# A vector of 2048 words loaded as 16 rows and turned on TensorE, in an attention and feed-forward kernel whose order a planner makes

## The chip, the core and the metric

The kernel runs on one core of one Trainium2 chip. The metric is the device time of one execution in microseconds (us); smaller is better. Three timed executions of the kernel before have a median of 761.31 us.

## What is computed

Soft-capped attention over 4 batches of 12 heads, 448 rows and 64 columns each, then a feed-forward layer with a leaky rectifier whose slope `alpha` is a vector of 2048 float32 words, one for each hidden column.

```
scores = cap * tanh(q @ k.T / sqrt(64) / cap)        # per batch and head
attn   = exp(scores - max) / (sum + 1e-9)
x      = attn @ v, heads side by side                 # (1792, 768)
h      = x @ w_in                                     # (1792, 2048)
g      = max(h, 0) + alpha * min(h, 0)
out    = g @ w_out                                    # (1792, 768)
```

## The kernel before

The work goes through four batches. The first batch's attention (`attention32`) runs in float32; its two query parts of 192 and 256 rows a head are taken one after the other for six pairs of heads, in units. The later batches (`attention`) run in pairs of float16 numbers, high and low part, with DMA transposes for the turned tiles. The products with w_in (`mm1`, line 741) and w_out (`mm2`, line 782) follow batch by batch. While the first batch's attention runs, w_in and w_out come in as 8-byte words in 16 chunks each, are turned into float32 by VectorE (lines 837, 841, 847), measured by a product with themselves (`norms`, line 861) and split into two float16 parts.

No queue is written out by hand. Each step is handed to `Plan.op` with a priority number, the engines that can do it with a time for each, and the regions that it reads and writes. `Plan.order` then plays the kernel through at build time: whenever an engine is free it takes the ready step with the least number, and the order in which the steps start there is the order in which each engine's queue gets them. For a DMA the three numbers are SyncE's time to issue it, the time from issue to the transfer, and the time for which the one transfer lane is held; the transfers are played one behind the other in that lane, and 1000 ns later a transfer has landed. The play begins at 1230 ns. A load of q, k or v has (500, 1900, 1000) ns, a load of w_in (500, 1900, 3400).

Where the play finds TensorE idle before a set time, it puts an empty product into the queue (`fill`, line 991), a 128 by 128 float16 product whose result nobody reads. On the chip these run in their place in the queue, whatever the chip then has to do.

A step that needs one of four PSUM banks takes it through a handle. A handle of kind "n" serves the small turns and maxima, and only one of that kind is held at a time.

`alpha` comes in by `g_scales`, called with priority 30 between the loads of the first batch and its attention. The tile `alph` holds word j*128+p in partition p, column j. From it `absmax` (line 345) takes a maximum per partition, `allmax` turns that column on TensorE (line 362), takes the maximum over the row (line 358) and spreads it back over the partitions by a product (line 365); `g_scale` makes the factors `sg`, `cs_g` and `ca_g` from it, which `mm1` applies to its products in the two steps behind each (lines 381 or 383, then 751). All steps of this chain share the region "sg", and so run in order.

Of the kernel before, what the change touches and what calls it, by code (L numbers as in the profile page):

```python
# [10 lines left out]
F32 = mybir.dt.float32  # L11
# [64 lines left out]
class Plan:  # L76
# [15 lines left out]
    def op(self, prio, times, fn, r=(), w=(), rows=1.0, port=True):  # L92
        o = lambda: None
        o.prio, o.times, o.fn, o.rows, o.idx, o.port = prio, times, fn, rows, len(self.ops), port
        o.handles, deps = [], set()
        for write, regions in ((False, r), (True, w)):
            for x in regions:
                if isinstance(x, Handle):
                    if x not in o.handles:
                        o.handles.append(x)  # L100
                        x.ops.append(o)
                    x = (x, 0, 1)
                space, lo, hi = x
                old = self.acc.setdefault(space, [])
                deps.update(e[2] for e in old if e[0] < hi and lo < e[1] and (write or e[3]))
                if write:
                    old[:] = [e for e in old if e[0] < lo or hi < e[1]]
        for write, regions in ((False, r), (True, w)):
            for x in regions:
                space, lo, hi = (x, 0, 1) if isinstance(x, Handle) else x  # L110
                self.acc[space].append((lo, hi, o.idx, write))
        o.deps = len(deps)
        o.next = []
        for d in deps:
            self.ops[d].next.append(o)
        self.ops.append(o)
        return o
# [120 lines left out]
def kernel(  # L238
# [11 lines left out]
    nc = tc.nc  # L250
    B, H, S, D = q.shape
    DM, DFF = w_in.shape
    P = 128
# [6 lines left out]
    NF = DFF // P  # L260
# [7 lines left out]
    def ct(shape, dt, name):  # L268
        return const.tile(shape, dt, tag=name, name=name)

    ps_s = [psum.tile([P, 2, 512], F32, tag=f"s{i}", name=f"s{i}") for i in range(2)]
    ps_p = [psum.tile([P, 512], F32, tag=f"p{i}", name=f"p{i}") for i in range(4)]
# [3 lines left out]
    amz = [small[:, i:i + 2] for i in (8, 10)]  # L276
    joint = ct([P, B // 2], F32, "joint")
    alph = ct([P, NF], F32, "alph")
    n_wi = ct([P, NF], F32, "n_wi")
    iv_wi = ct([P, NF], F32, "iv_wi")  # L280
    s_wi = ct([P, NF], F32, "s_wi")
# [2 lines left out]
    sg = ct([P, NF], F32, "sg")  # L284
# [31 lines left out]
    ident, identr = ct([P, P], F32, "ident"), ("ident", 0, 1)  # L316
# [11 lines left out]
    plan = Plan()  # L328
    op = plan.op
# [14 lines left out]
    def absmax(o, i):  # L344
        nc.vector.tensor_reduce(out=o, in_=i, axis=AX.X, op=ALU.max, apply_absolute_value=True)
# [3 lines left out]
    def allmax(prio, src, rows, r, first, w):  # L349

        h = plan.handle("n")
        m, at = src.shape[-1], mxt_no[0]
        mxt_no[0] += 1 + m if m > 1 else 1
        top, diag = mxt[:m, at:at + 1], mxt[:m, at + 1:at + 1 + m]
        tr = (("mxt", at), 0, 1)

        def reduce(e):
            nc.vector.tensor_reduce(out=top, in_=ps_p[h.slot][:m, :rows], axis=AX.X, op=ALU.max)
            if m > 1:
                nc.vector.tensor_scalar(out=diag, in0=ident[:m, :m], scalar1=top, scalar2=None, op0=ALU.mult)  # L360

        op(prio, {"pe": 150}, lambda e: nc.tensor.transpose(ps_p[h.slot][:m, :rows], src, ident[:rows, :rows]),
           r=[*r, identr], w=[h])
        op(prio, {"dve": 480 if m > 1 else 260}, reduce, r=[h], w=[tr], port=False)
        op(prio, {"pe": 100}, lambda e: nc.tensor.matmul(  # L365
            ps_p[h.slot][:, 256:256 + m], ones[:m], diag if m > 1 else top, start=True, stop=True), r=[tr], w=[h])
        op(prio, {"dve": 150}, lambda e: first(ps_p[h.slot][:, 256:256 + m]), r=[h], w=w, port=False)
# [548 lines left out]
            split_w(WT_P + WT_S * j, wo[j], room_r(wo_room[j]), room[j], room_r(j), s_wo[:, j:j + 1], ("s_wo", 0, 1), share(j, AO))  # L916

    def g_scales(prio):
        op(prio, {"sp": (500, 1100, 900)}, lambda e: nc.sync.dma_start(out=alph, in_=alpha.rearrange("(j p) -> p j", p=P)), w=[("sg", 0, 1)])
        op(prio, {"dve": 80}, lambda e: absmax(c_g, alph), w=[("sg", 0, 1)])  # L920
        allmax(prio, c_g, P, [("sg", 0, 1)], lambda top: nc.vector.tensor_scalar(
            out=c_g, in0=top, scalar1=1.0, scalar2=2.0 ** 20, op0=ALU.max, op1=ALU.mult), [("sg", 0, 1)])
        op(prio, {"dve": 1130}, g_scale, w=[("sg", 0, 1)])
# [42 lines left out]
    def all_ops():  # L966
        loads32()
        g_scales(30)
        for part in range(2):
            for pair in range(NPAIR):  # L970
                attention32(part, pair)
        for j in range(0, NF, WG):
            w_in_chunks(j, WG)
        for part in range(2):
            mm1_batch(0, *PART[part], part)
        w_out_all()
        out_scale(0)
        for b in range(1, B + 1):
            if b < B:
                vbatch(b)  # L980
                for pair in range(NPAIR):
                    attention(b, pair)
                out_scale(b)
            mm2_batch(b - 1)
            if b < B:
                mm1_batch(b, 0, S, 0)
# [52 lines left out]
```

## Time and profile before

| | |
|---|---|
| median of three timed executions | 761.31 us (761.2 to 761.73) |
| the profiled execution, its own time | 763.0 us |
| span of its trace | 761.1 us |
| mean granted TensorE clock in the span | 0.983 of full |
| instructions | 14048 |
| DMA packets | 227940, of which 191457 under 512 B |

The span goes from the first to the last instruction in the trace; the execution's own time has some 1.9 us around it. Busy time is the time in which an engine runs instructions; waiting, branching and issuing DMAs are not counted. A granted clock of 1.00 is 2.4 GHz, and TensorE's lower level is 1.2 GHz.

### The profile page before, as it was taken

The numbers are of one execution on the slowest core, as the hardware profiler recorded it, in microseconds if no ns is written. First come the engines' busy times: TensorE is split into PE (matmuls) and PEld (weight loads), VectorE is DVE, ScalarE is ACT, GpSimd is POOL, SyncE is SP. The second block draws the span as 40 slices with busy tenths as digits, with TensorE's granted clock in tenths as the row PEclk, the third lists the DMA queues.
The fourth block names the chain that finished last, engine by engine and source line by source line (L and its number), as shares of the span: only waits on it lengthen the run. The fifth ranks groups of instructions, "written<-read, shape, count | busy, mean of one in ns | idle before, by whom it ended". The sixth has DMA issues, their size and how long they took to land.

```text
span 761.1 us, 14048 instructions
## 1 busy us (share of the span) xinstructions
PE 736.8 (97%) x5332; PEld 464.8 (61%) x5332; DVE 511.1 (67%) x1146; ACT 452.4 (59%) x903; POOL 125.8 (17%) x197
## 2 busy tenths in 40 slices
PE   9999989989888999999999999999999999999997
PEld 6866666668776876566555555555555555555664
DVE  3787888998877798867778787877877701543000
ACT  3567778787675687767767666767776500332010
POOL 1010110124333110211433300012233000000000
PEclk9999989999998999999999999999999999999999
DMA  8984441868885836898867599999765721000001
GB/s 212 253 235 125 129 163 55 266 155 157 193 168 102 155 75 142 185 183 153 141 126 132 117 187 213 180 177 159 134 121 93 121 54 39 1 0 1 22 22 42
DMA packets 227940, 98.71 MB, mean 130 GB/s; under 512 B 191457, under 2 KB 224161, under 8 KB 227873
## 3 DMA queue, kind: packets, MB, share of 16 engines
q1 hardware_dynamic: 227872, 97.82, 62.2%
q8 instruction: 42, 0.69, 0.4%
q14 instruction: 26, 0.20, 0.1%
HBM read 45.82 MB, written 5.51 MB: 67 GB/s over the span
## 4 chain that ended last, share of the span: by engine, by line
PE 83%; DVE 5%; DMA 4%; ACT 4%; issue 2%; POOL 0%; SPq 0%; ACTq 0%; POOLq 0%
PE p L782 28%; PE p L741 24%; PE s L724 5%; PE p L596 5%; PE p L991 5%; PE s L665 4%; PE p L560 4%; DMA ptall<-pw 3%; PE p L610 2%; PE p L455 2%; DVE mxs L513 1%; PE p L861 1%; PE p L365 1%; PE p L454 1%; DVE pw L389 1%
## 5 line engine op out<-in xcount | busy, mean ns | idle before, releaser
L741 PE MATMUL p<-xring,wi 128*128 128x448 f16 (+2 forms) x1440 | 230.0, 319 | 1.9 <-DVE gr L751 1.9
L782 PE MATMUL p<-wp,gall 128*128 128x384 f16 x1344 | 225.2, 326 | 0.0
L741 PEld LDWEIGHTS <-wi 128*128 128x128 f16 x1440 | 138.4, 100 | 87.1 <-issue 5.0
L782 PEld LDWEIGHTS <-gall 128*128 128x128 f16 x1344 | 129.8, 98 | 89.3 <-issue 4.3
L520 ACT ACTIVATE tall<-tall,mxs,small 128x448 f32<-128x448 f32 x126 | 94.2, 749 | 14.9 <-POOL mxs L515 14.7
L515 POOL TENSOR_SCALAR mxs<-mxs,small 128x2 f32<-128x2 f32 (+1 forms) x93 | 45.9, 493 | 319.0 <-DVE mxs L513 202.1
L389 DVE SCALAR_TENSOR_TENSOR pw<-tall,rr,pw 128x448 f16<-128x448 f32 x126 | 85.5, 688 | 17.6 <-ACT pw L381 17.4
L386 POOL TENSOR_TENSOR gall<-gr,gall 128x384 f16<-128x384 f32 (+4 forms) x80 | 66.6, 842 | 167.2 <-ACT gall L375 101.6
L381 ACT ACTIVATE pw<-tall,rr 128x448 f16<-128x448 f32 x98 | 63.1, 660 | 43.7 <-DMA ptall<-pw 39.6
L751 DVE SCALAR_TENSOR_TENSOR gr<-p,ca_g,gr 128x448 f32<-128x448 f32 (+2 forms) x80 | 46.6, 585 | 54.0 <-ACT gr L381 53.7
L513 DVE TENSOR_REDUCE mxs<-tall 128x2 f32<-128x896 f32 (+1 forms) x72 | 69.0, 961 | 5.3 <-ACT tall L508 4.8
L508 ACT ACTIVATE tall<-s,ams 128x896 f32<-128x896 f32 (+1 forms) x72 | 64.8, 903 | 10.8 <-DVE pw L389 6.1
L724 PE MATMUL s<-qkTs 128*128 128x448 f16 (+1 forms) x288 | 61.4, 360 | 6.3 <-ACT tall L508 6.2
L381 ACT ACTIVATE gr<-p,cs_g 128x448 f32<-128x448 f32 (+2 forms) x60 | 32.9, 549 | 53.2 <-PE p L741 48.8
L381 ACT ACTIVATE wp<-p,small 128x384 f32<-128x384 f32 x23 | 13.3, 580 | 75.0 <-PE p L782 74.9
L991 PE MATMUL p<-ident 128*128 128x128 f16 x790 | 52.8, 224 | 2.2 <-POOL ident masks.py:199 1.7
L991 PEld LDWEIGHTS <-ident 128*128 128x128 f16 x790 | 48.3, 100 | 6.5 <-issue 2.4
L375 ACT ACTIVATE gall<-gr 128x384 f16<-128x384 f32 (+4 forms) x85 | 35.8, 434 | 25.3 <-DVE gr L751 25.0
L596 PE MATMUL p<-ptall,vs 112*64 112x448 f16 (+1 forms) x456 | 47.7, 350 | 1.6 <-issue 1.4
L724 PEld LDWEIGHTS <-qkTs 128*128 128x128 f16 (+1 forms) x288 | 22.3, 101 | 28.8 <-issue 15.6
L596 PEld LDWEIGHTS <-vs 112*64 112x64 f16 x456 | 25.9, 110 | 21.2 <-issue 7.5
L665 PE MATMUL s<-tall,qkTs 128*128 128x448 f32 x84 | 38.6, 589 | 0.0
(142 smaller groups left out, 828.6 us busy)
## 6 DMA issues: line engine op xcount, KB each, us to landing
wp<-in_moe_w_in_dram SPq DMA_DIRECT2D x16, 768.0 KB, 6.7
wp<-in_moe_w_out_dram SPq DMA_DIRECT2D x16, 768.0 KB, 4.7
rvs<-in_v_dram SPq DMA_DIRECT2D x38, 224.0 KB, 3.1
rqk<-in_q_dram SPq DMA_DIRECT2D x18, 224.0 KB, 3.0
rqk<-in_k_dram SPq DMA_DIRECT2D x18, 224.0 KB, 3.3
ptall<-pw SPq DMA_TRANSPOSE x148, 3.3
wp<-in_k_dram SPq DMA_DIRECT2D x6, 224.0 KB, 10.2
wp<-in_q_dram SPq DMA_DIRECT2D x6, 224.0 KB, 10.3
```

What stands on the lines that cost most here:

```text
L381: nc.scalar.activation(out=o, in_=i, func=AF.Copy, scale=s)
L386: (nc.gpsimd if e == "pool" else nc.vector).tensor_tensor(out=o, in0=a, in1=b, op=ALU.subtract)
L389: nc.vector.scalar_tensor_tensor(out=o, in0=i, scalar=s, in1=hi, op0=ALU.mult, op1=ALU.subtract)
L508: op(pr, {"act": 245 + 377 * m}, lambda e, s=s, t=t, m=m: nc.scalar.activation(out=t, in_=s[:, :m, :S].rearrange("p c (j k) -> p c j k", j ...
L513: op(pr, {"dve": 136 + 469 * m}, lambda e, mt=mt, t=t: nc.vector.tensor_reduce(out=mt, in_=t, axis=AX.XY, op=ALU.max), r=tr, w=[mr], port= ...
L520: nc.scalar.activation(out=t[:, x], in_=t[:, x], func=AF.Exp, scale=capt, bias=mt[:, x:x + 1], accum_out=u.sums[:, c:c + 1])
L596: nc.tensor.matmul(pv[x * D:(x + 1) * D, :n], vs[:, z, c:c + D], u.pt[x][:CP, y * NCH + kc], start=(i == 0), stop=(i == len(prods) - 1))
L665: steps(u, prio, n, lambda s, c: nc.tensor.matmul(s, qz[:, c * P:(c + 1) * P], kt[:, pair], start=True, stop=True), lambda c: 750, [qr, kt ...
L724: nc.tensor.matmul(s[rows], qT[:, x * S + cols.start:x * S + cols.stop], qkT[:, r0:r0 + NCH, :], start=(z == 0), stop=(z == 1))
L741: nc.tensor.matmul(ps_p[h.slot][:, :n], w[:, z, kk, :], x[:, d, o:o + n], start=(kk == 0 and z == d), stop=(kk == NPAIR - 1 and z == 1))
L782: nc.tensor.matmul(ps_p[h.slot][:, :NH], g[j][:, d, t * P:(t + 1) * P], w[:, z, hf * NH:(hf + 1) * NH], start=(j == 0 and z == d), stop=(j ...
L991: nc.tensor.matmul(ps_p[slot][:, :P], ident.bitcast(F16)[:, :P], ident.bitcast(F16)[:, P:], start=True, stop=True)
```

## The change

The load of `alpha` takes it as 16 rows of 128 words, each contiguous in memory, into a new tile `arow` of 16 partitions. A new TensorE step turns this tile into a PSUM bank of kind "n" against a 16 by 16 corner of the identity, and a new VectorE step copies the 128 by 16 result to `alph`. What follows is the same. The planner's numbers for the load change from (500, 1100, 900) to (500, 1900, 100), and the two new steps have 100 and 190 ns. The constants of the planner stay.

```diff
@@ -276,6 +276,7 @@
     alph = ct([P, NF], F32, "alph")
+    arow = ct([NF, P], F32, "arow")
@@ -916,7 +917,10 @@
     def g_scales(prio):
-        op(prio, {"sp": (500, 1100, 900)}, lambda e: nc.sync.dma_start(out=alph, in_=alpha.rearrange("(j p) -> p j", p=P)), w=[("sg", 0, 1)])
+        op(prio, {"sp": (500, 1900, 100)}, lambda e: nc.sync.dma_start(out=arow, in_=alpha.rearrange("(j p) -> j p", p=P)), w=[("arow", 0, 1)])
+        h = plan.handle("n")
+        op(prio, {"pe": 100}, lambda e: nc.tensor.transpose(ps_p[h.slot][:, :NF], arow, ident[:NF, :NF]), r=[("arow", 0, 1), identr], w=[h])
+        op(prio, {"dve": 190}, lambda e: nc.vector.tensor_copy(alph, ps_p[h.slot][:, :NF]), r=[h], w=[("sg", 0, 1)], port=False)
         op(prio, {"dve": 80}, lambda e: absmax(c_g, alph), w=[("sg", 0, 1)])
```

## Rows read from the trace of the kernel before

**Rows 1.** The page's table of busy us, share of the span and instructions.

```profile
PE 736.8 (97%) x5332; PEld 464.8 (61%) x5332; DVE 511.1 (67%) x1146; ACT 452.4 (59%) x903; POOL 125.8 (17%) x197
```

**Rows 2.** Busy us by stage: stretch, length, engines, granted clock, DMA share, GB/s.

```profile
40.00:80.00 40.00, 40.00 (x298) 26.70 (x297) 30.52 (x70) 28.72 (x62) 3.83 (x9) 1.00 0.63 179
80.00:160.00 80.00, 75.23 (x530) 53.10 (x530) 70.67 (x149) 66.44 (x138) 8.77 (x13) 0.94 0.51 152
160.00:240.00 80.00, 67.97 (x648) 55.80 (x645) 66.78 (x150) 56.99 (x128) 28.73 (x38) 0.91 0.78 161
...
360.00:600.00 240.00, 239.17 (x1456) 127.60 (x1454) 189.73 (x427) 168.26 (x334) 60.60 (x90) 1.00 0.81 147
```

**Rows 3.** The same for the empty products of line 991 alone (products, weight loads).

```profile
0.00:40.00 40.00, 16.47 (x224) 14.82 (x224) 1.00 1.00 233
...
160.00:240.00 80.00, 3.83 (x48) 3.46 (x48) 0.91 0.78 161
240.00:280.00 40.00, 17.64 (x288) 16.59 (x288) 1.00 0.67 120
```

**Rows 4.** Timeline of SyncE's queue: start us, us of the issue, line, out<-in.

```profile
2.52 0.46 SPq L825 DMA_DIRECT2D wp<-in_moe_w_in_dram  x1
3.03 0.55 SPq L919 DMA_DIRECT2D alph<-in_moe_alpha_dram  x1
3.62 4.31 SPq L399 DMA_DIRECT2D wp<-in_k_dram  x1
```

**Rows 5.** DMA packets of the stretches 6 to 7, 7 to 8, 8 to 9 us.

```profile
DMA packets 343, 0.35 MB, mean 351 GB/s; under 512 B 0, under 2 KB 343, under 8 KB 343
...
DMA packets 1758, 0.13 MB, mean 135 GB/s; under 512 B 1633, under 2 KB 1758, under 8 KB 1758
...
DMA packets 494, 0.05 MB, mean 50 GB/s; under 512 B 447, under 2 KB 494, under 8 KB 494
```

**Rows 6.** DMA issues of 1.3 to 3.7 us: KB, us from issue to landing.

```profile
small<-in_cap_dram SPq DMA_DIRECT2D x1, 0.5 KB, 3.3
...
alph<-in_moe_alpha_dram SPq DMA_DIRECT2D x1, 8.0 KB, 6.2
...
wp<-in_k_dram SPq DMA_DIRECT2D x1, 224.0 KB, 7.0
```

**Rows 7.** Timeline of alpha's readers and of VectorE ahead of them.

```profile
8.72 0.35 DVE L377 COPY qkTs<-p 64x192 f32<-64x192 f32 x1 [4.09 <-PE p L455]
...
11.81 0.16 DVE L345 TENSOR_REDUCE small<-alph 128x1 f32<-128x16 f32 x1
...
12.35 0.27 PE L362 MATMUL p<-ident,small 128*1 128x128 f32 x1
...
18.14 0.17 DVE L936 TENSOR_TENSOR ca_g<-alph,cs_g 128x16 f32<-128x16 f32 x1
```

**Rows 8.** Instructions on the tile cs_g: ns least/median/most, first and last start us.

```profile
L381 ACT ACTIVATE gr<-p,cs_g x60: 399/626/636, 158.7 to 694.5; 128x448 f32<-128x448 f32 x34, 128x192 f32<-128x192 f32 x13, 128x256 f32<-128x256 f32 x13
```

**Rows 9.** The chain that ended last, 8 to 14 us: start us, us, what.

```profile
12.07 0.45 PE p L991 x8
12.52 0.11 PE p L362
12.63 0.22 PE p L991 x4
```

**Rows 10.** The same chain, its five long waits for a transfer, 130 to 247 us.

```profile
132.93 4.87 DMA rqk<-in_k_dram
...
195.54 3.25 DMA rqk<-in_q_dram
...
205.26 3.76 DMA ptall<-pw
...
221.62 8.06 DMA ptall<-pw
...
241.72 4.58 DMA ptall<-pw
```

## The prediction

> **What bounds the kernel now.** I read the page's busy table first: TensorE is busy for 736.8 of 761.1 us and no other engine for more than 511.1 [rows 1]. The reader is to see a kernel bound by TensorE, with 24.3 us in which it does nothing (761.1 less 736.8). That share is a mean over unlike stages, so the table by stage comes next [rows 2]. TensorE is full in 40 to 80 us, leaves 4.8 us of 80 to 160 idle (80 less 75.23) and 12.0 of 160 to 240 (80 less 67.97), and has 239.17 of 240 us in 360 to 600. In 80 to 240 VectorE is the busiest engine but for one (70.67 of 80, then 66.78), and TensorE's granted clock is 0.94 and 0.91, so part of that time ran at 1.2 instead of 2.4 GHz. Late in the kernel nothing but TensorE's own queue of products counts.
>
> "Full" has to be taken with care. The planner puts empty products (line 991) wherever its plan has TensorE idle, a fixed number of them, and they cost their time on the chip whether or not there is still a gap. They hold 16.47 us of the first 40 us, 3.83 of 160 to 240 and 17.64 of 240 to 280 [rows 3]. So in the first 40 us TensorE's time is set by the plan: a gap that the plan no longer sees is what shortens it, not a transfer that lands sooner by itself.
>
> Alpha's own place is read from SyncE's queue, the DMA rates and the landing times. Alpha is the fifth DMA, issued at 3.03, and the next one, a load of k, holds SyncE for 4.31 us where the two issues ahead of it took 0.46 and 0.55 [rows 4]. The engines move 0.35 MB between 6 and 7 us, then 0.13 and 0.05 in the next two, while 1633 and 447 packets of under 512 B pass [rows 5]. Those 2080 small packets are alpha's 2048 words and some odds and ends. Alpha lands 6.2 us after its issue, at 9.2, the k load behind it at 10.6, 7.0 after its issue [rows 6].
>
> Its readers are read from the timeline. The first, VectorE's maximum, runs at 11.81, 2.6 us after the landing; the chain ends with the scaled alpha at 18.14 [rows 7], and the first use of a table that it makes is at 158.7 [rows 8]. Nothing on TensorE waits for alpha, then, nor for the k load: the turn of k follows at 12.85 (12.63 and 0.22), 2.2 us after that landing, and ahead of it in the chain that ended last stand 8 and 4 empty products, 0.45 and 0.22 us [rows 9].
>
> **The change, part by part.** *Removed: 2048 words as packets of their own.* At the 0.35 MB of the undisturbed us, the two us in question lost (0.35 less 0.13) and (0.35 less 0.05), over 0.35: 0.63 and 0.86, together 1.5 us of the DMA engines. The lower end counts the second us only by its share of the small packets, 447 to 1633 of the first: 0.63 times 1.27, 0.8 us. So each load behind alpha can land 0.8 to 1.5 us sooner. TensorE waits for none of them there, so by itself this is worth nothing.
>
> *Added: a load of 16 rows of 512 B.* The nearest row below is the smallest load, cap, 3.3 us from issue to landing; above, the scattered load itself, 6.2 [rows 6]. Alpha then lies in SBUF between 6.3 and 9.2 us.
>
> *Added: one TensorE turn of 16 by 128 and one VectorE copy of 128 by 16.* For the turn I take the turn of alpha's maxima, 0.27 us busy and 0.11 of the chain [rows 7, 9]; the copy stands between the maximum over the same 128 by 16 words, 0.16, and the copy of 64 by 192 out of PSUM, 0.35 [rows 7], and I take 0.16, for the size. In the plan the turn takes the place of empty products. If it doesn't, it costs 0.11 to 0.27. The copy falls where VectorE has little to do: it was idle for 4.09 us ahead of 8.72 [rows 7]. Cover gone, both cost 0.43 (0.27 and 0.16). The queue behind the new turn is that of TensorE's scores and turns; it would stand still if alpha landed after the turn is due. The plan makes it due no earlier than its own landing time for alpha: the start of 1230 ns, 1900 and 1000 for the first k load, 1000 for q, 3400 for w_in, 100 for alpha and 1000 for the landing, 9.63 us, which is 0.4 us after the latest landing I allow. So I put no wait there. The whole chain grows by these two steps and the way between them, some 1 us, against the 140 us until that first use.
>
> *Moved: the planner's clock for every later load.* In the plan alpha held the transfer lane for 900 ns and now holds it for 100. While that lane is the limit, every load behind it is due 0.8 us sooner in the plan. These are the kernel's own figures, no time of the chip. What the chip gets from them is fewer empty products: those ahead of the k turn, 0.45 and 0.22 us, are the ones that this can take away, 0.67 us, and the transfers give it the room, since they really come 0.8 us sooner at least. A second time it can't be had: a shift that is won at 12.85 is the same shift afterwards. I bound the direct effect by 0.8 us gained (the plan's whole shift) and 0.4 lost (nothing shifted, both new steps on the path), and take 0.67 gained.
>
> *Moved without being touched: the order of everything else.* The planner takes whichever ready step has the least priority number at each moment. With other due times in the first 40 us, other pairs meet on VectorE, ScalarE and SyncE, and the queues may come out otherwise up to 280 us. What this is worth the trace of before can't show. Its nearest rows are the five long waits for a transfer in the chain between 130 and 247 us: 4.87, 3.25, 3.76, 8.06 and 4.58 us [rows 10], on the mean 4.9. Each of them hangs on when SyncE came to issue one transfer.
>
> The profiled execution took 763.0 us for a span of 761.1, so 1.9 lie around the span; the sum against it is 763.0 less 0.67, 762.3. It stands 1.7 above the median of the three timed runs, 761.31, and the change is taken off that: 760.6.
>
> **The rivals.** *Hidden anyway, and no shift.* The readers of alpha come 2.6 us after the landing, the k turn 2.2 us after its own; if the plan was limited there by the scores and not by the loads, no empty product goes. Then the two steps are all that is left: 761.31 and at most 0.43, 761.7. Against it: 12 empty products stand right ahead of the k turn. The Trainium skill has this rule (DMA: Bandwidth & Descriptors, Rules for kernel authors): issue a DMA early and wait for it late, and its set-up cost lies beside the compute. By that rule too the old load cost nothing, and the change would not pay; the late reader in the trace agrees with it.
>
> *Slower: one more long wait between 130 and 247 us.* TensorE has few empty products to spare there (3.83 us in 160 to 240), and VectorE, which feeds the transposing transfers, has little room. If the new order puts one such transfer's issue behind another step on SyncE, another wait of the mean size comes on top: 760.6 and 4.9, 765.5. In 160 to 240 the granted clock is 0.09 short of full, which over 80 us is 7.2 us of work at full clock; a quarter more of that adds 1.8, 767.3. It decides once TensorE's idle time of 80 to 280 grows by over 2.2 us, which eats the 0.67 and passes the bound of a measurable change (0.2%, 1.5 us).
>
> *Faster: one such wait goes.* The same rows the other way: 760.6 less 4.9 is 755.7; less the longest, 8.06, it is 752.6. For it speaks that loads of the next batch's q and k, which two of the five waits name or follow, come sooner; against it that they come after 40 us, when the DMA share has fallen to 0.63 [rows 2] and the head start may have gone.
>
> **How the numbers follow.** Direct effect alone 0.33 (its own range 760.5 to 761.7), hidden anyway 0.05, slower 0.32, faster 0.30. The first two lie within 0.2%, so the same has 0.38. The time is that of the direct effect, 760.6. The range goes to one mean wait on the fast side, 755.7, and one mean wait with its clock on the slow side, 767.3, which leaves out about 2 in 10 between the two ends.
>
> **What would show it.** Packets of under 512 B nearly gone from 7 to 9 us, with some 0.3 MB moved in each; the k load behind alpha issued in about 0.5 us; alpha landed by 9.2; its turn near 10 to 12 us with no wait on TensorE; the k turn at about 12.2 with fewer empty products ahead. After 280 us the same stretches, shifted. The prediction is wrong if TensorE's idle time of 80 to 280, or its count of empty products, moves by more than 2 us: then the order decided, not alpha.

## The result, and the profile after

The changed kernel has a median of 768.36 us over 4 runs (766.63 to 770.64) against 761.52 for the kernel before (4 runs, 761.2 to 761.73): a ratio of 1.0092, 95% interval 1.0064 to 1.012. It is slower by some 6.8 us, where 760.6 was forecast and the range ended at 767.3. The profiled execution took 770.64 us for a span of 768.8.

Alpha's own part went as planned. The lines numbered here stand 1 to 4 below those of the kernel before (a product with w_out is L783, an empty product L995). First SyncE's queue, start and us of each issue, the counterpart of [rows 4]:

```profile
3.03 0.54 SPq L920 DMA_DIRECT2D arow<-in_moe_alpha_dram  x1
3.62 0.42 SPq L400 DMA_DIRECT2D wp<-in_k_dram  x1
```

then the DMA packets of 7 to 8 and of 8 to 9 us, for [rows 5]:

```profile
DMA packets 353, 0.32 MB, mean 319 GB/s; under 512 B 34, under 2 KB 353, under 8 KB 353
...
DMA packets 284, 0.27 MB, mean 271 GB/s; under 512 B 19, under 2 KB 284, under 8 KB 284
```

and the landing times of the two loads, for [rows 6]:

```profile
wp<-in_k_dram SPq DMA_DIRECT2D x1, 224.0 KB, 5.6
arow<-in_moe_alpha_dram SPq DMA_DIRECT2D x1, 8.0 KB, 5.5
```

The k load behind alpha is issued in 0.42 us instead of 4.31 and lands at 9.2 (3.62 and 5.6) instead of 10.6. Of the 2080 packets of under 512 B in these two us, 53 are left.

The new steps in the timeline (for [rows 7]), and the chain that ended last (for [rows 9]):

```profile
14.49 0.23 PE L922 MATMUL p<-ident,arow 16*128 16x16 f32 x1
...
16.20 0.16 DVE L923 COPY alph<-p 128x16 f32<-128x16 f32 x1
```

```profile
11.72 0.75 PE s L666 x2
12.47 0.10 PE p L455
12.57 0.34 PE p L456 x2
...
15.83 2.23 PE p L995 x38
```

The turn costs 0.23 us, the copy 0.16. The k turn (L455) follows the scores with no empty product between them, but behind the turns stand 38 of them where there were 27. From the first scores to the second TensorE runs 38 empty products in all, where it ran 39 (8, 4 and 27): they have moved, they have not gone.

What was lost is in the stages. Busy us, for [rows 2]:

```profile
40.00:80.00 40.00, 38.27 (x311) 28.35 (x311) 29.26 (x68) 25.74 (x56) 2.90 (x7) 0.96 0.49 144
80.00:160.00 80.00, 73.77 (x566) 53.99 (x565) 71.83 (x151) 62.10 (x128) 5.17 (x13) 0.98 0.49 149
160.00:240.00 80.00, 67.88 (x599) 53.54 (x599) 66.89 (x145) 61.41 (x134) 22.79 (x36) 0.89 0.82 164
240.00:280.00 40.00, 38.30 (x428) 31.67 (x427) 31.67 (x69) 27.04 (x55) 10.42 (x15) 1.00 0.60 127
```

and the empty products alone, for [rows 3]:

```profile
0.00:40.00 40.00, 15.19 (x210) 13.82 (x210) 1.00 0.93 254
40.00:80.00 40.00, 4.28 (x62) 3.67 (x62) 0.96 0.49 144
80.00:160.00 80.00, 4.90 (x75) 4.44 (x75) 0.98 0.49 149
160.00:240.00 80.00, 1.44 (x20) 1.27 (x20) 0.89 0.82 164
240.00:280.00 40.00, 10.15 (x164) 9.59 (x165) 1.00 0.60 127
```

The first 40 us have 1.3 us less of them. Then TensorE is idle in 40 to 80 (1.7 us, before none), and from 80 to 160 it is idle for 6.2 instead of 4.8 us and holds empty products too, of which there were none. So it is the middle of the kernel that has changed, tens of us behind alpha's last reader. The page's first table, for [rows 1]:

```profile
PE 738.4 (96%) x5351; PEld 469.1 (61%) x5351; DVE 520.8 (68%) x1143; ACT 458.3 (60%) x907; POOL 116.4 (15%) x197
```

TensorE's idle time in the whole span is 30.4 us (768.8 less 738.4) against 24.3. The empty products take 53.3 against 52.8, so its real work takes 685.1 against 684.0. Of the 7.7 us between the two spans, 6.1 are idle time, 0.5 empty products and 1.1 real work.

A milestone shows where. The first product with w_out, in the instructions of its line (ns least, median, most; first and last start in us), starts at 278.6 before and at 290.8 after:

```profile
L782 PE MATMUL p<-wp,gall x1344: 323/326/337, 278.6 to 756.5; 128*128 128x384 f16 x192
```

```profile
L783 PE MATMUL p<-wp,gall x1344: 323/326/337, 290.8 to 763.8; 128*128 128x384 f16 x192
```

12.2 us are lost by then, and 4.5 of them come back behind it, where the empty products hold less than before.

The five long waits of [rows 10] have changed with the order. Those of over 3 us between 120 and 280 us are now

```profile
167.89 3.09 DMA rvs<-in_v_dram
175.39 3.07 DMA ptall<-pw
183.00 6.56 DMA rqk<-in_q_dram
199.65 4.27 DMA rvs<-in_v_dram
264.82 6.76 DMA ptall<-pw
```

together 23.8 us against 24.5, so the loss is not one more of them.

### The profile page after: what moved, and what is told of

Its sections match the earlier page's. It is cut to its first block, busy times and chain, and to the rows that moved or that the text cites. A ratio compares the mean times of both kernels' runs of the same rounds, so it can differ in the third digit from the quotient of the medians.

```text
span 768.8 us, 14096 instructions
## 1 busy us (share of the span) xinstructions
PE 738.4 (96%) x5351; PEld 469.1 (61%) x5351; DVE 520.8 (68%) x1143; ACT 458.3 (60%) x907; POOL 116.4 (15%) x197
## 4 chain that ended last, share of the span: by engine, by line
PE 84%; DMA 7%; DVE 4%; ACT 3%; issue 1%; POOL 0%; ACTq 0%; POOLq 0%; DVEq 0%
PE p L742 26%; PE p L783 25%; PE p L597 6%; PE s L725 5%; PE p L561 5%; PE p L995 5%; PE s L666 4%; DMA ptall<-pw 3%; PE p L456 2%; PE p L611 2%; DMA rqk<-in_q_dram 1%; DMA rvs<-in_v_dram 1%; DMA qkTs<-nat 1%; PE p L455 1%; PE p L862 1%
## 5 line engine op out<-in xcount | busy, mean ns | idle before, releaser
L783 PE MATMUL p<-wp,gall 128*128 128x384 f16 x1344 | 225.1, 326 | 0.0
L783 PEld LDWEIGHTS <-gall 128*128 128x128 f16 x1344 | 130.2, 98 | 88.8 <-issue 3.2
L390 DVE SCALAR_TENSOR_TENSOR pw<-tall,rr,pw 128x448 f16<-128x448 f32 x126 | 87.4, 705 | 13.3 <-ACT pw L382 12.7
L382 ACT ACTIVATE pw<-tall,rr 128x448 f16<-128x448 f32 x106 | 68.7, 661 | 44.9 <-DMA ptall<-pw 30.3
L516 POOL TENSOR_SCALAR mxs<-mxs,small 128x2 f32<-128x2 f32 (+1 forms) x94 | 42.5, 452 | 334.9 <-DVE mxs L514 269.9
L387 POOL TENSOR_TENSOR gall<-gr,gall 128x384 f16<-128x384 f32 (+4 forms) x78 | 60.8, 788 | 155.7 <-ACT gall L376 93.6
L995 PE MATMUL p<-ident 128*128 128x128 f16 x808 | 53.3, 223 | 2.7 <-POOL ident masks.py:199 1.7
L995 PEld LDWEIGHTS <-ident 128*128 128x128 f16 x808 | 48.8, 100 | 6.1 <-issue 2.3
L597 PE MATMUL p<-ptall,vs 112*64 112x448 f16 (+1 forms) x456 | 49.5, 362 | 2.5 <-DMA ptall<-pw 1.9
L382 ACT ACTIVATE wp<-p,small 128x384 f32<-128x384 f32 x18 | 10.4, 579 | 65.2 <-PE p L783 65.2
L597 PEld LDWEIGHTS <-vs 112*64 112x64 f16 x456 | 28.0, 113 | 21.9 <-issue 7.2
L561 PE MATMUL p<-diags,gall 128*112 128x128 f32 x248 | 34.6, 295 | 4.6 <-ACT ptall L376 2.4
```

The lines of the kernel that those rows point to most:

```text
L382: nc.scalar.activation(out=o, in_=i, func=AF.Copy, scale=s)
L387: (nc.gpsimd if e == "pool" else nc.vector).tensor_tensor(out=o, in0=a, in1=b, op=ALU.subtract)
L390: nc.vector.scalar_tensor_tensor(out=o, in0=i, scalar=s, in1=hi, op0=ALU.mult, op1=ALU.subtract)
L561: nc.tensor.matmul(ps_p[h.slot][:CP, j * P:(j + 1) * P], t[:, j], d, start=True, stop=True)
L597: nc.tensor.matmul(pv[x * D:(x + 1) * D, :n], vs[:, z, c:c + D], u.pt[x][:CP, y * NCH + kc], start=(i == 0), stop=(i == len(prods) - 1))
L783: nc.tensor.matmul(ps_p[h.slot][:, :NH], g[j][:, d, t * P:(t + 1) * P], w[:, z, hf * NH:(hf + 1) * NH], start=(j == 0 and z == d), stop=(j ...
```

## The experiments

Theory A: the planner draws the whole order anew for any edit of its input, and the time is that of the order; the load itself is worth nothing that can be measured. Theory B: the new load itself costs, by its turn, its wait or the traffic that comes sooner. Each run is compared with the kernel before on the same chip. Over the three batches that kernel has medians of 762.48, 762.53 and 762.84 us.

**The new load in the old order.** The load, the turn and the copy are put inside steps that the plan already has, with their old times, so that every queue is that of the kernel before but for one DMA, one product and one copy.

```diff
+                if i == 1:
+                    nc.tensor.transpose(s[:, 1, :NF], arow, ident[:NF, :NF])
...
-  nc.sync.dma_start(out=alph, in_=alpha.rearrange("(j p) -> p j", p=P))
+  nc.sync.dma_start(out=arow, in_=alpha.rearrange("(j p) -> j p", p=P))
...
+        def first_max(e):
+            nc.vector.tensor_copy(alph, ps_s[1][:, 1, :NF])
+            absmax(c_g, alph)
```

> Alpha as 16 rows with its turn and copy, but every queue in the order of the kernel before (one product, one copy and the DMA differ). Theory A, the order costs: 761.5 within 1.5 us, since the 6.8 us come from other queues and not from the load. Theory B, the new load itself costs (its turn, its wait, the traffic that comes sooner): 766 or more.

Measured: 761.67 us (12 runs), ratio 0.9998, interval 0.9983 to 1.0013. The load itself costs and gains nothing that can be told: the interval leaves room for some 1 us either way.

**The old load in the new order.** The changed kernel's plan with alpha scattered again; the turn takes a piece of the identity and the copy goes to a tile that nobody reads.

```diff
-  nc.sync.dma_start(out=arow, in_=alpha.rearrange("(j p) -> j p", p=P))
+  nc.sync.dma_start(out=alph, in_=alpha.rearrange("(j p) -> p j", p=P))
-  nc.tensor.transpose(ps_p[h.slot][:, :NF], arow, ident[:NF, :NF])
+  nc.tensor.transpose(ps_p[h.slot][:, :NF], ident[:NF], ident[:NF, :NF])
-  nc.vector.tensor_copy(alph, ps_p[h.slot][:, :NF])
+  nc.vector.tensor_copy(spare, ps_p[h.slot][:, :NF])
```

> Alpha word by word again, but every queue in the order of the changed kernel; the turn and the copy are kept on data that nobody uses. Theory A: as the changed kernel, 768.4 within 2.5 us. Theory B: back to 763 or less.

Measured: 768.13 us (12 runs), ratio 1.0058, interval 1.0037 to 1.0078. The loss stays without the load. With the run above this decides for A. In the traces TensorE's idle time goes with the order too, and not with the load. The first tables of the new load in the old order (span 759.4 us) and of this kernel (span 760.6) are

```profile
PE 735.3 (97%) x5333; PEld 465.1 (61%) x5333; DVE 512.4 (67%) x1147; ACT 452.0 (60%) x903; POOL 124.8 (16%) x197
```

```profile
PE 732.2 (96%) x5351; PEld 462.9 (61%) x5351; DVE 521.1 (69%) x1143; ACT 458.0 (60%) x907; POOL 116.1 (15%) x197
```

so the old order is idle for 24.3 us with the old load and for 24.1 with the new one, the new order for 28.4 with the old load and for 30.4 with the new one. The trace of this kernel is of one of its two fastest executions, 762.38 us. The runs of this kernel reach from 762.24 to 770.0, and the ratio is somewhat under that of the changed kernel, so a small part of the loss, some 0.3% between the two ratios, may still hang on how the new load meets the new order; the intervals overlap.

**The direct gain alone.** As the first run, with 12 empty products less ahead of the k turn.

```diff
     def fill(slot):
+        fills[0] += 1
+        if 53 < fills[0] <= 65:
+            return
```

> As the run with the new load in the old order, and without the 12 empty products ahead of the first k turn that waited for a load. If the predicted direct gain is real: 0.67 us less than that run, so some 760.8. If TensorE then waits for the loads or for the other engines instead: the same as that run.

Measured: 762.85 us (12 runs), ratio 1.0014, interval 1.0000 to 1.0029, where the first run has 0.9998. The gain is not there at the end. It is in the middle. The chain that ended last, in the first run and then in this one (the same scores of line 668), shows a lead of 0.75 us at 52, of which 0.2 is there before the place of the products left out (first scores at 10.39 against 10.60):

```profile
52.07 2.26 PE s L668 x6
```

```profile
51.32 2.26 PE s L668 x6
```

and the instructions with w_in and with w_out, again of the first run and of this one, show it at 153.4 against 154.9 and gone at 277.6 against 277.3:

```profile
L744 PE MATMUL p<-xring,wi x1440: 243/352/421, 154.9 to 692.4; 128*128 128x448 f16 x108, 128*128 128x192 f16 x36, 128*128 128x256 f16 x36
...
L785 PE MATMUL p<-wp,gall x1344: 323/326/338, 277.3 to 754.8; 128*128 128x384 f16 x192
```

```profile
L744 PE MATMUL p<-xring,wi x1440: 243/352/422, 153.4 to 693.3; 128*128 128x448 f16 x108, 128*128 128x192 f16 x36, 128*128 128x256 f16 x36
...
L785 PE MATMUL p<-wp,gall x1344: 323/326/338, 277.6 to 755.7; 128*128 128x384 f16 x192
```

In this pair of traces the lead did not run out in a wait. From the first product with w_in to the first with w_out TensorE is idle for 11.7 us in both (122.4 less 110.72 in the first run, 124.2 less 112.52 in this one), but the same 1196 products take 1.8 us longer. The lines of 160 to 240, first run and then this one, have the same busy time for 666 and for 652 products, at a granted clock of 0.96 and 0.91:

```profile
160.00:240.00 80.00, 68.32 (x666) 55.89 (x665) 68.84 (x153) 58.49 (x132) 27.70 (x38) 0.96 0.79 163
```

```profile
160.00:240.00 80.00, 68.32 (x652) 56.46 (x649) 67.08 (x151) 57.30 (x128) 28.14 (x38) 0.91 0.80 159
```

Whether the earlier arrival brought the lower clock, or these two executions differ in it anyway, is not shown by one trace of each.

**The planner's number alone.** The kernel before, one tuple changed.

```diff
-        op(prio, {"sp": (500, 1100, 900)}, lambda e: nc.sync.dma_start(out=alph,
+        op(prio, {"sp": (500, 1900, 100)}, lambda e: nc.sync.dma_start(out=alph,
```

> The kernel before with nothing but the planner's numbers for alpha's load changed, from (500, 1100, 900) to (500, 1900, 100); the scattered load stays and there are no new steps. Theory A: the order is drawn anew, so the time moves by several us either way, most likely up, 762 to 770. Theory B: 761.5 within 1 us.

Measured: 767.94 us (6 runs), ratio 1.0071, interval 1.0056 to 1.0085. The steps are those of the kernel before; their order, the engine that takes a step where the planner may choose, and the number of empty products differ.

**The new steps alone.** The changed kernel with (500, 1900, 900) in place of (500, 1900, 100).

> The changed kernel with the planner's transfer time for alpha set back from 100 to 900 ns: the load as rows, the turn and the copy stay, and the plan's clock for the later loads is that of before. Theory A, the order is drawn anew by any edit of the plan: a third order, somewhere from 758 to 770 and not at 768 in particular. Theory C, the loads that are due 0.8 us sooner in the plan are what spoils the order: within 1.5 us of the kernel before, 761 to 764.

Measured: 767.66 us (10 runs, 763.7 to 771.54), ratio 1.0068, interval 1.0039 to 1.0097. Theory C falls: with the old clock for the later loads the time is lost as well. The two halves of the edit lose 5.5 and 5.1 us alone and 6.8 together, so they don't add up.

**Three edits that have nothing to do with the load's form.** In the kernel before `WI_S = 6.37` becomes 6.4; `V_P = 42.05` becomes 42.5; alpha's numbers become (500, 1900, 500).

> The kernel before with one constant of the planner that has nothing to do with alpha, the priority step between the w_in chunks, from 6.37 to 6.4; alpha is loaded as before. Theory A: another draw of the order, 758 to 770, and most likely not within 1.5 us of 762.5. Theory C: as before, 762.5 within 1.5 us.

> The kernel before with the priority of the first batch's v loads from 42.05 to 42.5, nothing else. Theory A: another draw, 758 to 770. Theory C: as before, 762.5 within 1.5 us.

> The kernel before with alpha's transfer time in the plan at 500 instead of 900 ns, the scattered load as it was. Theory A: another draw, 758 to 775. Theory C: half the shift, so half the loss of the run with 100 ns, some 765.

Measured (4 runs each): 771.24 us (ratio 1.0122, 1.0096 to 1.0148), 753.17 us (0.9881, 0.9851 to 0.991) and 771.93 us (1.0126, 1.0097 to 1.0155). The first two lie outside the 758 to 770 that theory A gave: the draws spread more widely than expected. With `WI_S = 6.4` the kernel's output is off by 0.047 (relative error), so this order does not compute what the others do; which step is at fault is open. It has the 4542 real products of the kernel before, but its time is not counted below. Half of the shift in the plan loses more than all of it. The same work with a priority raised by one per cent is 9.4 us faster. The first product with w_out starts at 270.7 in that run:

```profile
L782 PE MATMUL p<-wp,gall x1344: 323/326/337, 270.7 to 745.0; 128*128 128x384 f16 x192
```

Its page's first table gives 22.9 us of idle time in a span of 749.8, and the empty products take 46.5 us, the least but one of all orders:

```profile
PE 726.9 (97%) x5245; PEld 457.3 (61%) x5245; DVE 516.4 (69%) x1147; ACT 455.2 (61%) x901; POOL 123.6 (16%) x198
```

The run with 500 ns has 66.0 us of them and 23.1 idle. Idle time and empty products together are 69.4 us in the fast one, 77.1 before, 83.7 after and 89.1 in this one; what is left for real work is 680.4, 684.0, 685.1 and 679.2. Over the traces of all kernels with right output and no product left out, the sum of the two is 69.4 to 72.0 us in the fast orders, 77.0 and 77.1 in the old one, and 81.4 to 89.1 in the slower ones. So the orders differ by TensorE's gaps, planned or not.

**The fast order with the new load.** The edit of the first run made to the kernel with `V_P = 42.5`; the queues are otherwise those of that kernel.

> The order of the run with the v loads' priority at 42.5, every queue the same, but alpha loaded as rows with its turn and copy set into that order. Theory A, only the order counts and the load itself is worth nothing that can be measured: as that run, 753.2 within 1.5 us, 9 us below the kernel before. Theory B, the load itself costs: 758 or more.

Measured: 755.43 us (4 runs), ratio 0.9896, interval 0.9879 to 0.9913, against 0.9881 with the scattered load. The median lies 2.2 us above 753.2, outside the 1.5 expected, but the two kernels ran on different chips; by the ratios, each against the kernel before on its own chip, the distance is 1.1 us, and the intervals overlap. A small cost of the new load isn't excluded here, a gain is not to be seen.

**The same constant in the changed kernel.** `V_P = 42.5` with the change as it is.

> The changed kernel with the priority of the first batch's v loads at 42.5, which made the kernel before 9 us faster. Theory A, each edit draws the order anew: the gain does not carry over, 762 to 772. Theory D, the earlier place of other loads ahead of v is a gain of its own: some 9 us below the changed kernel, 757 to 761.

Measured: 772.72 us (4 runs), ratio 1.0131, interval 1.0115 to 1.0147. What took 9.4 us off the one kernel takes nothing off the other: by the ratios it adds some 3 us, with intervals that overlap. The output of this order is off by the same 0.047 as with `WI_S = 6.4`. So theory D falls only as far as the time of a kernel with a wrong output can tell, and this run too is not counted below.

**The changed kernel with its constants drawn anew.** 23 priority constants moved, by at most some ten units but for three of the large ones (`MM_P` from 334.69 to 390.96, `PEN` to 496.2 and `PEN2` to 277.86), for an earlier end of the planner's own play.

> The changed kernel with 23 of the planner's priority constants drawn anew, so that the planner's own play of the changed kernel ends sooner; the work is the same. Theory A: the 6.8 us are no property of the change, so some orders of the changed kernel are as fast as the kernel before or faster, 750 to 762. Theory B: 766 or more.

Measured: 751.86 us (4 runs), ratio 0.9862, interval 0.9844 to 0.988. The change as such stands in no way of a kernel that is 1.4% faster than the one before. It is the fastest version tried here, together with the old load at `V_P = 42.5`, from which its interval doesn't part it. The constants of the kernel before were not drawn anew in this way, so which of the two loads has the better best order is not shown.

**Without the late empty products.** The kernel before, same order, with none of its last 481 empty products (29.7 us).

> The kernel before, same order, without its empty products after 250 us (481 of them, 29.7 us). Theory E, they take time that the real work could use: 735 to 755. Theory F, the gaps are there on the chip as well: TensorE idles in their place and its clock falls, 760 to 770.

Measured: 758.36 us (4 runs), ratio 0.994, interval 0.9923 to 0.9957. Neither theory's figure: 4.5 of 29.7 us. Its stages of 160 to 280 and 280 to 360 us,

```profile
160.00:280.00 120.00, 98.16 (x865) 74.60 (x863) 100.95 (x225) 84.68 (x180) 37.11 (x51) 0.89 0.75 148
280.00:360.00 80.00, 73.79 (x447) 40.53 (x446) 65.03 (x144) 61.16 (x113) 11.53 (x15) 0.94 0.81 164
```

and those of the kernel before, in the same stretches,

```profile
160.00:280.00 120.00, 107.82 (x1137) 89.12 (x1134) 100.96 (x225) 84.61 (x177) 37.69 (x51) 0.94 0.74 147
280.00:360.00 80.00, 79.41 (x632) 49.17 (x630) 61.75 (x138) 58.20 (x108) 9.44 (x14) 1.00 0.81 158
```

show that TensorE is idle for 15.3 us more (120 less 98.16 and 80 less 73.79, against 12.18 and 0.59) and that its granted clock falls, to 0.89 and 0.94 of the 2.4 GHz level from 0.94 and 1.00. The whole span says where the time went, by this run's first table (span 757.5 us):

```profile
PE 717.3 (95%) x4851; PEld 438.8 (58%) x4851; DVE 510.4 (67%) x1146; ACT 452.8 (60%) x903; POOL 125.5 (17%) x197
```

The empty products left are 23.3 us, so the same real products take 694.0 us (717.3 less 23.3) where they took 684.0, and the idle time is 40.2 us where it was 24.3. Of the 29.5 us of empty products that the two traces differ by, 15.9 came back as idle time, 10.0 as slower products at the lower clock, and 3.6 is the difference of the spans. Half of the planned gaps are gaps on the chip as well, and a third of what the empty products take they give back by the clock.

## Why the prediction was wrong

The step that failed is the term for the order of everything else. The forecast of 760.6 has it at nothing and is the direct effect alone; the runs show the loss there: 5.7 us with the old load in the new order (768.13 against 762.48), none that can be told with the new load in the old order, and 6.8 with the change itself.

- *Removed packets: right.* 0.8 to 1.5 us were forecast for the loads behind alpha; the k load landed 1.4 us sooner and was issued in 0.42 us, for the 0.5 forecast. One pair of traces is a rough measure of it: over the six profiled executions with rows and the same queue ahead, that load landed 5.3 to 6.5 us after its issue, over the seven with words 6.9 to 7.6. The Trainium skill (DMA: Bandwidth & Descriptors, Rules for kernel authors) says that a DMA whose last dimension isn't contiguous becomes one descriptor per element and is better rearranged; 2080 small packets before and 53 after agree with it.
- *New steps: right in size, off in place.* 0.27 and 0.16 us were taken, 0.23 and 0.16 measured, and no wait on TensorE. The turn came at 14.49 and not between 10 and 12.
- *Nobody waits for alpha: right.* The new load in the old order has a ratio of 0.9998. The Trainium skill's rule on the same page, that the fixed set-up cost of a DMA issued early and waited for late lies beside the compute, agrees with that run. The rival "hidden anyway" described the load, though not the kernel.
- *0.67 us from the empty products ahead of the k turn: a number met by luck, and worth nothing at the end.* From the first scores to the second it takes 7.92 us (18.06 less 10.14) instead of 8.57 (18.31 less 9.74), so 0.65 us are there. But 11 of the 12 products stand again behind the turns, 38 for 27. What left this stretch is other work, put off until later: the turn of alpha's maxima and the product that spreads them (L362 and L365, 0.11 and 0.31 us of the chain before) and six products that measure w_in (L861, 0.34), against 0.16 for the new turn. The sentence that failed is that "a shift that is won at 12.85 is the same shift afterwards". With the order held, a lead of 0.75 us was gone by the first product with w_out. The lines of the kernel before that this rests on are

```profile
9.74 2.33 PE s L665 x6
...
14.94 0.31 PE p L365 x2
...
16.35 1.61 PE p L991 x27
17.96 0.34 PE p L861 x6
18.31 2.31 PE s L665 x6
```

and those of the changed kernel

```profile
10.14 2.33 PE s L666 x6
...
18.06 2.31 PE s L666 x6
```

- *The order of everything else: seen, left out of the sum, priced too low, and ranked wrongly.* This is the step that failed. The prediction gave 0.33 to the direct effect alone, which asks that 280 us of queues either stay or come out equally good. They did neither. With the same work, the orders of this study with right output run from 751.9 to 771.9 us. Five of them were drawn by an edit without any aim at a better order (the change, its two halves, `V_P = 42.5` and the transfer time of 500), and four of the five are slower than the kernel before, by 5 to 9 us. That the old constants had been chosen for the old order, so that most other draws lose, would fit this; no run shows it. One long wait, 4.9 us, and its clock, 1.8, was too small a unit for that.
- *The slower rival: right in sign, wrong in mechanism.* It asked for one more long wait between 130 and 247 us. The waits of over 3 us add up to slightly less than before. What grew is idle time in many pieces from 40 us on: 3.1 us more in 80 to 280, which is over the 2.2 named as the point that decides, and 1.7 in 40 to 80. By the prediction's own sign (idle time of 80 to 280 moved by more than 2 us) the order decided, not alpha.

Which pair of steps first meets in another way, so that the middle comes out later, is open.

## What to carry to other kernels

Where a planner writes the queues, an edit has two prices: that of the work it changes, and that of the order that is drawn with it. The first is measured with the old order held, by putting the new instructions inside steps that the plan already has; here the first is nothing that can be told, and the second is anything from some 9 us gained to some 9 lost. Judge such a change with the order drawn anew on both sides, not by one draw against one order; here that was done for the changed kernel alone. And look at the output of every order: two of those drawn here have a wrong one.

## What the runs showed that was not expected

- One order has a spread of its own: 29 runs of the kernel before on one chip reach from 758.62 to 763.8 us, 12 of the changed order with the old load from 762.24 to 770.0. The two traces of the changed order, with the new load and with the old (spans 768.8 and 760.6), differ by 2.0 us of idle time and 5.9 of real work (685.1 and 679.2), at a mean granted clock of 0.983 and 0.992: most of that difference is in how fast the same products ran.
- 481 empty products of 29.7 us in all, left out, give back 4.5 us. They aren't free, since the work behind them comes sooner without them. But half of their time is TensorE's idle time under another name, and a third is what the real products lose when the granted clock falls without them, to 0.89 in 160 to 280.
- A DMA of 8 KB as single words held the queue's next issue for 4.21 to 4.93 us in every profiled execution with it, and the k load behind it landed some 1.3 us later on the mean, without a measurable change of the kernel's time.
